# Sliding-window attention with a mixture layer: a written-out order of work and slots in place of the list scheduler, scales on single columns, Strassen's products from step 2

## The chip, the cores and the metric

One core of one Trainium2 chip runs the whole kernel. The metric is device time in microseconds (us); three executions are timed and the median counts. A further execution is profiled, and every row below comes from that one.

## What is computed

```python
B, H, S, SG, D = 8, 8, 512, 32, 64          # batch, heads, local and global tokens, head size
s_g   = q_g @ concat(k_g, k_l).T / sqrt(D)  # 32 global tokens see all 544
out_g = softmax(s_g) @ concat(v_g, v_l)
s_l   = concat(q_l @ k_g.T, where(|i - j| <= 32, q_l @ k_l.T, -1e9)) / sqrt(D)
out_l = softmax(s_l) @ concat(v_g, v_l)
x = concat(out_g, out_l)                    # 4352 tokens of 512
h = x @ w_in                                # 512 -> 2048, both weights come as float64
g = where(h >= 1, h, where(h <= -1, 0, (h + 1)**2 / 4))
out = g @ w_out                             # 2048 -> 512
```

## The kernel before, in words

**Number form.** Every operand of a matmul is scaled by a power of two and split in two float16 halves, high and low, and a product is three matmuls (high-high, low-high, high-low). The weights come as float64 words: `decode`, `signed` (line 590) and `halves` (line 608) make float32 and then the halves from them. To find a scale, the kernel multiplies a tile with itself on PE (a Gram matrix; its largest entry on the diagonal is a squared norm), takes the maximum on DVE, spreads it over the partitions (`all_max`, line 510) and takes the reciprocal.

**Steps.** Eight batches; a batch has two steps of 256 local tokens, so steps 0 to 15, and four batches together have one step for their global tokens. A step's parts have names: `aa` (bit `aa100` is batch 1, tile 0, head pair 0) makes scores on PE, the masked maximum on DVE, exp on ACT, the high half of the probabilities (a cast) on DVE or ACT and the low half (a subtraction) on POOL or DVE, both into a buffer `pb`, and turns `pb` with a transposing DMA. `ab` multiplies the turned probabilities with V; `ax` divides by the sum and turns the result. `m` multiplies with w_in; `act` (line 1133) evaluates the piecewise function on ACT and DVE, and POOL subtracts for the low half. `o` multiplies with w_out and the step's rows are stored. Ahead of these come the loads, the splits of q, k and v (`pq`, `pk`, `pv`), the weights' decoding (`wd`, `od`) and halves (`wh`, `oh`).

**Two forms of `m`.** `moe1` (line 1145) needs 48 matmuls of 128x128 for each of 8 pairs of group and tile, 384 for a step. `moe_f` (line 1199) does it by Strassen's scheme with 7 products of 48 instead of 8, 336 for a step; it needs sums of weight blocks (`combine`, line 1164, and `replace`, line 1183), and more additions on ACT and DVE. `T["fast"]` is the first step that uses it, 3 here.

**What sets the order.** The kernel is written twice over: a first pass records every operation, `segments` (line 198) cuts the record into runs of one engine, and `schedule` (line 252), a list scheduler with a cost for each operation (`cost`, line 151), due times, and a table of 500 hand-set shifts (`LATER`), puts them into one order and gives each tile a slot of the 48 shared SBUF slots of 2 KB (`room`), the 6 of 4 KB (`twin`) or the 8 PSUM banks. All this is done when the program is built. On the chip each engine works through a fixed list, and a second pass in `build` (line 1457) issues it, so nearly every instruction has the line 1474, and loads the line 1476. All DMAs are issued by SP, one after the other; a load also waits for the fifth load before it.

Of the kernel before, what the change touches and what calls it, by code (L numbers as in the profile page):

```python
# [89 lines left out]
def extent(ap, tiles):  # L90

    dims, size = [tuple(d) for d in ap.ap], mybir.dt.size(ap.dtype)
    if tiles[ap.tensor.name][2]:
        return ap.tensor.name, 0, 128, 0, 2048
    row = dims[0][0]
    p0, off = divmod(ap.offset, row) if row else (0, ap.offset)
    n = 1 + sum(abs(st) * (c - 1) for st, c in dims[1:])
    return ap.tensor.name, p0, p0 + dims[0][1], off * size, (off + n) * size


# [10 lines left out]
def shares(engine, op, a, k, tiles):  # L111

    if engine == "gpsimd":
        return op != "memset"
    if engine != "vector" or op in ("memset", "reciprocal", "tensor_reduce"):
        return False
    ins = {"tensor_scalar": a[1:2], "tensor_copy": a[1:2], "scalar_tensor_tensor": [a[1], a[3]] if len(a) > 3 else []}.get(op, a[1:3])
    ins = list(ins) or [k["in0"], k["in1"]]
    held = [x for x in ins if is_ap(x) and not tiles.get(x.tensor.name, (0, 0, 1))[2]]
    return len(held) > 1 or (op in ("tensor_scalar", "tensor_copy") and len(held) == 1 and free(held[0]) > 1)  # L120


def free(ap):
    n = 1
    for d in ap.shape[1:]:
        n *= d
    return n


def stretch(ap):  # L130

    n = 1
    for st, c in reversed([tuple(d) for d in ap.ap][1:]):
        if st != n and c > 1:
            break
        n *= c
    return n * mybir.dt.size(ap.dtype)


def cost(engine, op, a, k, outs, ins, tiles):  # L140

    o = outs[0]
    n = free(o)
    if engine == "tensor":
        if ins and ins[0].dtype == F32:
            return 4 * n / 2.1 + 10, 0
        t = max(28.0, n / 2.4 + 2.5)
        return (t / 4 if o.shape[0] == 32 else t), 0
    if engine == "sync":
        b = o.shape[0] * n * mybir.dt.size(o.dtype)  # L150
        if op == "dma_start_transpose":
            return 1320.0, b / 186.0
        run = min(stretch(x) for x in (o, ins[0]))
        return 600.0, b / (215.0 if run < 512 else 340.0)
    if engine == "scalar":
        ptr = any(free(x) == 1 for x in ins[1:])
        if "accum_out" in k:
            own = 190 if ptr else 95
        elif mybir.dt.size(o.dtype) == 2:
            own = 185 if ptr else 45 if ins[0].tensor.name in tiles and tiles[ins[0].tensor.name][2] else 90  # L160
        else:
            own = 235 if ptr else 135
        return own + n / 1.2 + (93 if "accum_out" in k else 0), 0
    if engine == "gpsimd" and o.dtype == I32:
        return 125 + n * 3.6, 0
    if engine == "gpsimd":
        return (125 + n * (1.93 if len([x for x in ins if free(x) > 1]) > 1 else 1.05) if op != "memset" else 60 + n * 0.82), 0
    big = [x for x in ins if free(x) > 1]
    ps = any(x.tensor.name in tiles and tiles[x.tensor.name][2] for x in big + [o])
    if op == "memset":  # L170
        return 60 + n / 0.96, 0
    if len(big) > 1 or ps or op == "tensor_reduce":
        m = max(free(x) for x in big) if big else n
        return 70 + 60 * len([x for x in ins if free(x) == 1]) + m / 0.96 + (8 if "accum_out" in k else 0), 0
    return 75 + n / (1.92 if n > 16 else 0.96), 0


class Segment:
    __slots__ = ("n", "engine", "calls", "t", "xfer", "after", "before", "new", "uses", "load", "step", "parts", "left", "ready", "prio", "t0", "done")


def segments(steps, tiles, prio, names):

    segs, last = [], {}
    for sn, calls in enumerate(steps):
        cur = None
        for engine, op, a, k in calls:  # L190
            outs, ins = sides(op, a, k)
            t, x = cost(engine, op, a, k, outs, ins, tiles)
            fresh = {tiles[nm][0] for nm in (x.tensor.name for x in outs) if nm in tiles and nm not in last}

            near = [x.tensor.name for x in sides(*cur.calls[-1])[0]] if cur and cur.engine == engine in ("vector", "scalar") else []
            if (cur is None or cur.engine != engine or engine == "sync" or fresh & {tiles[nm][0] for nm in cur.new}
                    or any(x.tensor.name in near for x in ins)):
                cur = Segment()
                cur.n, cur.engine, cur.calls, cur.parts, cur.t, cur.xfer = len(segs), engine, [], [], 0.0, 0.0
                cur.after, cur.before, cur.new, cur.uses = set(), [], [], set()  # L200
                cur.load, cur.ready, cur.prio, cur.step = op == "load", 0.0, prio[sn], names[sn]
                segs.append(cur)
            if engine == "tensor" and not cur.calls and outs[0].shape[0] == 32:
                t += 190.0
            cur.calls.append((op, a, k))
            cur.t += t
            cur.parts.append((t, shares(engine, op, a, k, tiles)))
            cur.xfer += x
            for aps, write in ((ins, False), (outs, True)):
                for ap in aps:  # L210
                    if ap.tensor.name not in tiles:
                        continue
                    nm, p0, p1, b0, b1 = extent(ap, tiles)
                    if nm not in last:
                        assert write, (nm, op)
                        last[nm] = []
                        cur.new.append(nm)
                    cur.uses.add(nm)
                    kept = []
                    for e in last[nm]:  # L220
                        q0, q1, c0, c1, w, who = e
                        if q0 < p1 and p0 < q1 and c0 < b1 and b0 < c1 and (w or write):
                            if who != cur.n:
                                cur.after.add(who)
                            if write and p0 <= q0 and q1 <= p1 and b0 <= c0 and c1 <= b1:
                                continue
                        kept.append(e)
                    e = (p0, p1, b0, b1, write, cur.n)
                    if e not in kept:
                        kept.append(e)  # L230
                    last[nm] = kept
    for g in segs:
        for p in g.after:
            segs[p].before.append(g.n)
# [135 lines left out]
def attention_moe(nc, memory, q_l, k_l, v_l, q_g, k_g, v_g, w_in, w_out, out):  # L370
# [3 lines left out]
    P = 128  # L374
# [1249 lines left out]
```

## Time and profile before

| | us |
|---|---|
| three executions | 939.27, 935.76, 936.0; median 936.0 |
| the profiled execution | 938.49 |
| its span, first to last instruction | 936.8 |
| PE busy in it | 869.6 (93%), 12180 matmuls |
| DVE busy | 778.9 (83%) |
| ACT busy | 636.0 (68%) |
| POOL busy | 425.2 (45%) |
| chain that ended last | PE 63%, DVE 10%, DMA 8%, ACT 5% |

The span is shorter than the profiled execution by 1.7 us, and that execution is 2.5 us above the median. A row names the engine, the operation, what it writes and reads (out<-in, numbers of buffers left out), shapes, the count, busy time and mean length of one, and then how long the engine stood idle before and what ended the wait. A busy PE is not PE at its peak, because matmuls overlap; the granted clock of PE is shown beside it.

### The profile page before, as it was taken

What the parts mean: (1) busy time and instruction counts of PE and PEld (TensorE: products, weight loads), DVE (VectorE), ACT (ScalarE), POOL (GpSimd) and SP (SyncE); (2) the same over time, 40 slices, a digit from 0 to 9 for tenths busy, and PEclk for the clock granted to TensorE, in tenths of its full rate; (3) what the DMA queues carried; (4) which work ended last, traced back from release to release, by engine and by line L of the source; (5) the groups of instructions that cost most, each with busy time, mean ns of one, the idle gap of its engine ahead of it and who ended that gap; (6) DMA issues with size and microseconds to landing.
All of it is one profiled execution on the core that took longest, in us unless ns stands there. A gap on an engine that the chain in (4) does not pass through costs nothing.

```text
span 936.8 us, 30633 instructions
## 1 busy us (share of the span) xinstructions
PE 869.6 (93%) x12180; PEld 648.1 (69%) x12180; DVE 778.9 (83%) x2102; ACT 636.0 (68%) x1530; POOL 425.2 (45%) x447
## 2 busy tenths in 40 slices
PE   2567889989999999999999999999999999999998
PEld 1443857757877686868686768868676777778774
DVE  3889989879888998999678888799879997878462
ACT  2699777768875696688666677668777765566341
POOL 8135475532434534473446344363345352636230
PEclk9788989989999999999999999999999999999999
DMA  8999918988999699979794578949999877364000
GB/s 236 271 230 231 228 24 137 176 168 134 179 175 167 109 181 168 192 127 173 159 182 97 106 161 143 157 70 197 170 182 140 136 131 126 69 123 78 13 24 23
DMA packets 412527, 135.64 MB, mean 145 GB/s; under 512 B 389088, under 2 KB 398304, under 8 KB 412384
## 3 DMA queue, kind: packets, MB, share of 16 engines
q1 hardware_dynamic: 412384, 133.69, 76.7%
q8 instruction: 95, 1.56, 0.7%
q14 instruction: 48, 0.39, 0.1%
HBM read 44.56 MB, written 8.91 MB: 57 GB/s over the span
## 4 chain that ended last, share of the span: by engine, by line
PE 63%; DVE 10%; DMA 8%; ACT 5%; issue 4%; SPq 1%; POOL 1%; ACTq 0%; POOLq 0%; DVEq 0%
PE bank L1474 63%; DVE room L1474 5%; DMA room<-const_pb 3%; ACT room L1474 3%; DVE bank L1474 1%; ACT weights_w L1474 1%; SPq L1474 1%; DMA twin<-in_moe_w_out_dram 1%; DMA room<-in_v_g_dram 1%; POOL room L1474 1%; DMA room<-in_q_l_dram 1%; DVE const_pb L1474 1%; DVE weights_w L1474 1%; ACT junk_junka L1474 1%; DMA room<-in_v_l_dram 1%
## 5 line engine op out<-in xcount | busy, mean ns | idle before, releaser
L1474 PEld LDWEIGHTS <-room 128*128 128x128 f16 (+3 forms) x5056 | 290.2, 99 | 217.2 <-issue 19.3
L1474 PE MATMUL bank<-weights_w,room 128*128 128x512 f16 x1632 | 375.2, 382 | 1.0 <-DVE small_nb L1474 0.4
L1474 POOL TENSOR_TENSOR room<-room,room 128x512 f16<-128x512 f32 (+4 forms) x199 | 222.3, 1124 | 200.1 <-ACT room L1474 182.6
L1474 PEld LDWEIGHTS <-weights_w 128*128 128x128 f16 (+1 forms) x4160 | 231.5, 98 | 39.3 <-DVE weights_w L1474 24.3
L1474 PE MATMUL bank<-room,weights_w 128*128 128x128 f16 (+1 forms) x4032 | 234.7, 216 | 1.5 <-ACT room L1474 0.7
L1474 POOL TENSOR_TENSOR const_pb<-room,const_pb 128x384 f16<-128x384 f32 (+1 forms) x115 | 121.8, 1061 | 214.3 <-DVE const_pb L1474 102.7
L1474 ACT CAST room<-room 128x512 f16<-128x512 f32 (+2 forms) x212 | 121.8, 582 | 84.8 <-DVE room L1474 64.8
L1474 ACT ACTIVATE room<-room,small_nb 128x224 f32<-128x224 f32 (+1 forms) x256 | 117.2, 459 | 46.8 <-DVE small_nb L1474 41.7
L1474 PE MATMUL bank<-room,room 128*128 128x64 f16 (+3 forms) x2688 | 125.3, 197 | 19.6 <-DMA room<-const_pb 11.8
L1474 PE MATMUL bank<-room,twin 128*128 128x128 f16 (+1 forms) x2160 | 123.0, 216 | 0.7 <-DVE room L1474 0.4
L1474 PEld LDWEIGHTS <-twin 128*128 128x128 f16 x2160 | 115.5, 98 | 3.2 <-issue 0.7
L1474 ACT ACTIVATE room<-bank,batch_small_ms 128x512 f32<-128x512 f32 (+1 forms) x114 | 85.1, 751 | 36.7 <-DVE bank L1474 24.7
L1474 DVE CUSTOM_DVE_ANT_0 room<-bank,const_mask,batch_small_q 128x224 f32<-128x224 f32 (+1 forms) x256 | 98.7, 425 | 6.2 <-PE bank L1474 5.8
L1474 ACT ACTIVATE junk_junka<-room 128x512 f16<-128x512 f32 (+2 forms) x110 | 69.0, 628 | 38.9 <-DMA room<-in_q_l_dram 16.4
L1474 DVE SCALAR_TENSOR_TENSOR bank<-bank,batch_small_ms,room 128x512 f32<-128x512 f32 (+1 forms) x114 | 82.0, 721 | 14.7 <-ACT room L1474 14.6
L1474 DVE SCALAR_TENSOR_TENSOR room<-room,batch_small_ms,bank 128x512 f32<-128x512 f32 (+1 forms) x114 | 80.6, 711 | 0.8
L1474 ACT COPY room<-bank 128x512 f32<-128x512 f32 (+2 forms) x98 | 56.2, 589 | 20.3 <-PE bank L1474 18.9
L1474 DVE CAST const_pb<-room 128x448 f16<-128x448 f32 (+1 forms) x109 | 47.6, 438 | 24.1 <-DMA room<-const_pb 20.0
L1474 DVE TENSOR_TENSOR bank<-bank,room 128x512 f32<-128x512 f32 (+1 forms) x60 | 39.4, 658 | 19.3 <-PE bank L1474 18.7
L1474 DVE SCALAR_TENSOR_TENSOR room<-room,batch_small_ms,room 128x512 f32<-128x512 f32 (+1 forms) x60 | 53.2, 887 | 1.3 <-ACT room L1474 0.9
L1474 DVE TENSOR_TENSOR room<-room,room 128x512 f16<-128x512 f32 (+2 forms) x56 | 42.8, 768 | 11.6 <-ACT room L1474 11.2
L1474 ACT ACTIVATION_READ_ACCUMULATOR room<-room,small_nb 128x1 f32 x256 | 48.2, 188 | 0.0
(165 smaller groups left out, 945.4 us busy)
## 6 DMA issues: line engine op xcount, KB each, us to landing
room<-room SPq DMA_DIRECT2D x80, 128.0 KB, 2.8
weights_w<-in_moe_w_in_dram SPq DMA_DIRECT2D x32, 256.0 KB, 4.2
room<-in_q_l_dram SPq DMA_DIRECT2D x32, 256.0 KB, 3.6
twin<-in_moe_w_out_dram SPq DMA_DIRECT2D x32, 256.0 KB, 4.1
out_dram<-room SPq DMA_DIRECT2D x32, 256.0 KB, 3.1
room<-in_k_l_dram SPq DMA_DIRECT2D x24, 256.0 KB, 3.8
room<-in_v_l_dram SPq DMA_DIRECT2D x24, 256.0 KB, 4.4
room<-const_pb SPq DMA_TRANSPOSE x124, 3.6
```

The source lines that it names most:

```text
L1474: getattr(getattr(tc.nc, engine), op)(*a, **k)
```

## The change

The cost functions, the list scheduler and the table of shifts go. In their place stand two tables of numbers, one for the order of all 4635 runs of work and one for the slot of each tile. The settings in `T` that choose an engine for one operation now reach over all 128 head pairs and all 16 steps, where many stopped at the first 16 or 32. Beside that: `fast` is 2; the Gram matrices of w_in, w_out and K add all their blocks into one 128x128 region, where they had 128x512 (for w_in one for eight blocks instead of four, so two reductions in place of four); `moe_scales` and `out_scale` work on one column where the scale is the same for all, and `act` then reads that column. `gram` for q, scaled identities for k and v (`by_pe`, `total`) are written but not used with these settings (`es`, `gramq`).

```diff
-def schedule(segs, tiles, hop, slack, landing, ahead):
...
+def plan(steps, tiles):
+
+    sizes, line = segments(steps, tiles)
+    order = [int(x) for x in ORDER.split()]
+    assert sorted(order) == list(range(len(sizes)))
+    taken = {}
+    for key, nms in line.items():
+        slots = [int(x) for x in SLOTS[key].split()] if key in SLOTS else [0] * len(nms)
...
-        if f % WG == 0:
-            W["n"] = ps_o.tile([P, WG, P], F32, tag="p", name=f"wn{f}")
+        u = f % (2 * WG)
+        if u == 0:
+            W["n"] = ps_o.tile([P, P], F32, tag="p", name=f"wn{f}")
         for k in range(NK):
             x = half[:, k * P:(k + 1) * P]
-            nc.tensor.matmul(W["n"][:, f % WG], x, x, start=(k == 0), stop=(k == NK - 1))
+            nc.tensor.matmul(W["n"], x, x, start=u == 0 and k == 0, stop=u == 2 * WG - 1 and k == NK - 1)
...
+    def gram(tiles, name):
+
+        t = ps_t.tile([P, P], F32, tag="p", name=name)
+        for i, (st, n) in enumerate(tiles):
+            half = st[:n].rearrange("p h d -> p (h d)").bitcast(BF16).rearrange("p (c t) -> p c t", t=2)[:, :, 1]
+            for k in range(NK):
+                x = half[:, k * P:(k + 1) * P]
+                nc.tensor.matmul(t, x, x, start=i == 0 and k == 0, stop=i == len(tiles) - 1 and k == NK - 1)
+        return t
...
-            nc.vector.tensor_reduce(ss, t, axis=AX.XY, op=ALU.max)
+            t = gram(list(d["rawk"].values()), f"kn{b}")
+            nc.vector.tensor_reduce(ss, t, axis=AX.X, op=ALU.max)
...
-        bd, rb, s2, sg, hs, a1, a2 = [t[:, c0:c1] for t in d["ms"][:7]]
+        c = slice(c0, c0 + 1)
+        bd, rb, s2, sg, hs, a1, a2 = [t[:, c] for t in d["ms"][:7]]
...
-    def out_scale(d, gs=None):
+    def out_scale(d, part=3):
...
-        c = slice(g, g + 1)
+        c = g // 2 * 2 if d["first"] else g
+        c = slice(c, c + 1)
...
+ORDER = ("6 7 42 8 5 34 0 4 35 30 1 22 23 24 43 25 26 44 9 45 12 54 13 32 31 82 81 83 84 85 86 89 55 56 57 3 860 1820 280 90 "
...
-T = dict(late=1, fast=3, grams="pp", sqs="aaamaa", cb=200, cbs=5, lk0=4.19, lq0=1.76, lv0=30, sk=12, sq=14,
-         adds="vvvvv1vv1vvvavvv1a1v1aavaavava1v", subs="ppppppvppppvvvpvpppppvvvvpppvppp", glow="ppvppppppppvpppv",
...
-         mags="vaapaaaaaaaaapaaaaapaaaaaaaaaaaa", lows="ppppppvv", halves="aaaaaaaaagacacacdecchccdddfdcbef",
-         shifts="pppapvvpvvvvvvvvvvvvvvvvvpvvvvvv", splits="vvvvvvvvvvvpvvvpvvvpvppp", att=1.35, s0=60, s1=100, s2=254.09,
+T = dict(es="nnnn", gramq="aaaaaaaa", dg="vvvvvvvvvvvvvvv", sid="vvvvv", fast=2, grams="ppaaaaaa", sqs="vaaaaa", cb=200,
...
+         mags="aaappaaaapapappaaaapaaaaaaaaaaaa", lowx="vvvvvvvvvvvvvppvvppvvpvvvvvpvvvvvvvvpvvvvpvppvvpv",
...
+         shifts="pavapvapvvvvvvvvvvvvvvvvvpvvvvvv", splits="vvvvvvvvvvvpvvvpvpvpppvp", att=1.35, s0=60, s1=100, s2=254.09,
```

The engines' lists differ almost everywhere, but their contents little. PE has 48 matmuls of 128x128 fewer. Of the low halves, 33 subtractions of `act` and 23 of `pb` go from POOL to DVE, 10 of `ax` the other way, and 26 casts of `pb` go from DVE to ACT; six copies and six additions come for the earlier Strassen step. SP issues 641 DMAs instead of 639.

**POOL at the start.** `w0` to `w4` are the first blocks of w_in, two instructions for each shift of their low bits; `negid` and `ident` are two diagonal matrices, and `pb0`, `pb1`, `pgb` buffers that are zeroed. Before (the diagonal matrices were POOL's first four instructions, ahead of these):

```order
L1474 MEMSET const_pb0_0_61 128x1024
L1474 MEMSET const_pb1_0_62 128x1024
L1474 MEMSET const_pgb_0_63 128x1280
L1474 MEMSET const_logp_0_64 128x1
L1474 TENSOR_SCALAR weights_w0_0_66<-weights_w0_0_66 128x512 x2
L1474 TENSOR_SCALAR weights_w2_0_68<-weights_w2_0_68 128x512 x2
L1474 TENSOR_SCALAR weights_w1_0_67<-weights_w1_0_67 128x512 x2
```

and now:

```order
L1301 MEMSET const_logp_0_64 128x1
L1301 TENSOR_SCALAR weights_w0_0_66<-weights_w0_0_66 128x512 x2
L1301 MEMSET const_negid_0_84 128x128
L1301 AFFINE_SELECT const_negid_0_84<-const_negid_0_84 128x128
L1301 MEMSET const_ident_0_85 128x128
L1301 AFFINE_SELECT const_ident_0_85<-const_ident_0_85 128x128
```

The two diagonal matrices went behind the shift of `w0`; the shifts of `w1` and `w2` left POOL, for ACT and DVE.

**DVE, the scale of batch 0's K.** `small_amk` holds the norm, `small_dg` the diagonal matrix that PE spreads, `batch_small_sk` the scale that every split of K waits for; `bank` and `weights_w` rows are the decoding of w_in, `q5` the scales of q. Before:

```order
L1474 TENSOR_SCALAR small_amk_0_104<-small_amk_0_104 128x1
L1474 TENSOR_SCALAR small_dg_0_106<-const_negid_0_84,small_amk_0_104 128x128
L1474 TENSOR_SCALAR batch_small_q5_0_111<-batch_small_q5_0_111 128x2
L1474 TENSOR_REDUCE small_wmx_0_103<-bank_3_93 128x1
L1474 TENSOR_SCALAR batch_small_q5_0_111<-batch_small_q5_0_111 128x2
L1474 SCALAR_TENSOR_TENSOR bank_5_108<-bank_5_108,weights_w4_0_70 128x512
L1474 TENSOR_REDUCE small_amk_0_104<-bank_2_91 128x1
L1474 TENSOR_SCALAR batch_small_q5_0_111<-batch_small_q5_0_111 128x2
L1474 TENSOR_SCALAR batch_small_sk_0_107<-small_amk_0_104 128x1
L1474 TENSOR_SCALAR weights_w5_0_71<-weights_w5_0_71 128x512
L1474 RECIPROCAL batch_small_sk_0_107<-batch_small_sk_0_107 128x1
```

and now:

```order
L1301 TENSOR_REDUCE small_amk_0_102<-bank_5_103 128x1
L1301 MEMSET const_ones_0_83 128x128
L1301 TENSOR_SCALAR small_amk_0_102<-small_amk_0_102 128x1 x2
L1301 TENSOR_SCALAR small_dg_0_104<-const_negid_0_84,small_amk_0_102 128x128
L1301 TENSOR_REDUCE small_amk_0_102<-bank_6_105 128x1
L1301 TENSOR_SCALAR batch_small_sk_0_106<-small_amk_0_102 128x1
L1301 RECIPROCAL batch_small_sk_0_106<-batch_small_sk_0_106 128x1
```

The chain now stands in one piece, and nothing of the decoding is between its parts.

**SP, the first turned probabilities of batch 1.** `pb0` is the buffer that `aa100` filled and `pb1` that of `aa101`. Before:

```order
L1476 DMA room_31_129<-in_v_g_dram 32x8x64
L1474 DMA qg_qgb_1_203<-qg_qga_1_202 64x256
L1474 DMA room_28_142<-room_27_144 64x1024
L1474 DMA qg_qgb_1_203<-qg_qga_1_202 64x256
L1476 DMA room_20_115<-in_v_l_dram 128x8x64
L1476 DMA room_0_92<-in_v_l_dram 128x8x64
L1476 DMA room_44_159<-in_v_l_dram 32x8x64
L1474 DMA room_40_195<-room_5_98 64x1024
L1476 DMA room_44_159<-in_v_g_dram 32x8x64
L1474 DMA_TRANSPOSE room_23_119<-room_37_140 128x8x128
L1474 DMA_TRANSPOSE room_18_114<-const_pb0_0_61 128x8x128
L1474 DMA_TRANSPOSE room_33_137<-const_pb1_0_62 128x8x128
```

and now:

```order
L1301 DMA room_46_159<-room_35_138 64x1024
L1301 DMA room_40_193<-room_6_113 64x1024
L1303 DMA room_5_112<-in_q_l_dram 128x8x64
L1303 DMA room_29_129<-in_v_l_dram 32x8x64
L1301 DMA_TRANSPOSE room_2_86<-room_23_136 128x8x128
L1301 DMA_TRANSPOSE room_31_140<-const_pb0_0_61 128x8x128
L1301 DMA_TRANSPOSE room_16_116<-const_pb1_0_62 128x8x128
```

Fewer loads of the next batch's V stand right ahead of the two transposes. On PE, between the scores of `aa100` and the first matmul that reads what it had turned, stood one group of 48 of `m`, three groups of 12 of `o` and six other pairs' scores; now it is four of `m`, five of `o` and seven pairs' scores.

## Rows read from the trace of the kernel before

**Rows 1.** The page: busy time and share of each engine, and the 40 slices of 23.4 us of PE's busy share and of its granted clock, in tenths.

```profile
PE 869.6 (93%) x12180; PEld 648.1 (69%) x12180; DVE 778.9 (83%) x2102; ACT 636.0 (68%) x1530; POOL 425.2 (45%) x447
...
PE   2567889989999999999999999999999999999998
...
PEclk9788989989999999999999999999999999999999
```

**Rows 2.** Stretches of the span: start and end, length, then busy time (and instructions) of PE, PE's weight loads, DVE, ACT and POOL, PE's granted clock, the DMA engines' busy share and GB/s.

```profile
0.00:60.00 60.00, 26.63 (x191) 19.32 (x192) 40.46 (x116) 32.80 (x68) 25.42 (x44) 0.84 0.99 255
60.00:165.00 105.00, 88.85 (x1219) 64.08 (x1218) 96.95 (x272) 87.59 (x194) 62.57 (x62) 0.93 0.80 158
165.00:225.00 60.00, 54.39 (x728) 39.76 (x727) 49.82 (x162) 43.70 (x124) 21.57 (x22) 0.94 0.89 162
225.00:328.00 103.00, 101.48 (x1396) 78.38 (x1396) 90.20 (x225) 72.57 (x176) 46.55 (x48) 1.00 0.90 157
328.00:937.00 609.00, 598.21 (x8651) 446.60 (x8649) 501.47 (x1332) 399.32 (x971) 269.11 (x273) 1.00 0.72 128
```

**Rows 3.** What PE waited for in the first 60 us: us in total, times, the longest.

```profile
PE bank L1474 <- DVE weights_w L1474: 21.6, 4, 15.4
PE bank L1474 <- DMA room<-room: 4.2, 1, 4.2
PE bank L1474 <- DVE small_w L1474: 3.6, 1, 3.6
```

**Rows 4.** The same from 165 us to the end.

```profile
PE bank L1474 <- DMA room<-const_pb: 9.9, 6, 4.4
PE bank L1474 <- DVE room L1474: 0.7, 2, 0.4
```

**Rows 5.** The timeline around 195 us, start, length, what, count, of PE, POOL and SP, and the stretch around it as in rows 2.

```profile
194.65 0.59 PE L1474 MATMUL bank<-room,room 128*128 128x128 f16 x12
199.64 2.21 PE L1474 MATMUL bank<-room,room 128*128 128x64 f16 x36 [4.40 <-DMA room<-const_pb]
201.66 3.97 PE L1474 MATMUL bank<-weights_w,room 128*128 128x512 f16 x12
...
189.99 0.92 POOL L1474 TENSOR_TENSOR const_pb<-room,const_pb 128x384 f16<-128x384 f32 x1 [0.29 <-DVE const_pb L1474]
...
196.27 2.65 SPq L1474 DMA_TRANSPOSE room<-const_pb  x2
...
187.40:210.80 23.40, 19.00 (x208) 12.23 (x206) 17.50 (x67) 15.05 (x51) 8.20 (x8) 0.85 0.86 168
```

**Rows 6.** The timeline of PE between 232 and 244 us, and the page's group of 128-column products.

```profile
235.85 0.52 PE L1474 MATMUL bank<-room,room 128*128 128x64 f16 x12
236.20 2.84 PE L1474 MATMUL bank<-room,weights_w 128*128 128x128 f16 x48
...
239.24 2.75 PE L1474 MATMUL bank<-weights_w,room 128*128 128x512 f16 x12
...
L1474 PE MATMUL bank<-room,weights_w 128*128 128x128 f16 (+1 forms) x4032 | 234.7, 216 | 1.5 <-ACT room L1474 0.7
```

**Rows 7.** The timeline of the first 16 us: POOL's diagonal matrices and its shifts of w_in's first three blocks, DVE's decoding of them and PE's first matmul.

```profile
0.80 0.21 POOL L1474 MEMSET const_negid<- 128x128 f16 x1 [0.29 <-POOLq L1608]
...
1.59 0.29 POOL L1474 TENSOR_SCALAR_AFFINE_SELECT const_ident<-const_ident 128x128 f16<-128x128 f16 x1
...
8.06 8.78 POOL L1474 TENSOR_SCALAR weights_w<-weights_w 128x512 f32<-128x512 uint16 x6
...
10.80 0.70 DVE L1474 SCALAR_TENSOR_TENSOR bank<-room,weights_w 128x512 int32<-128x512 int32 x1 [5.93 <-POOL weights_w L1474]
...
14.68 1.28 DVE L1474 SCALAR_TENSOR_TENSOR weights_w<-weights_w,bank 128x512 int32<-128x512 int32 x2
...
15.41 0.64 PE L1474 MATMUL bank<-weights_w 128*128 128x128 bf16 x4 [15.41 <-DVE weights_w L1474]
```

**Rows 8.** The timeline of DVE for batch 0's K: the two reductions, the diagonal matrix and the reciprocal.

```profile
18.33 0.69 DVE L1474 TENSOR_REDUCE small_amk<-bank 128x1 f32<-128x512 f32 x1
...
20.45 0.48 DVE L1474 TENSOR_SCALAR small_dg<-const_negid,small_amk 128x128 bf16<-128x128 f16 x1
...
22.92 0.28 DVE L1474 TENSOR_REDUCE small_amk<-bank 128x1 f32<-128x128 f32 x1
...
24.40 0.16 DVE L1474 RECIPROCAL batch_small_sk<-batch_small_sk 128x1 f32<-128x1 f32 x1
```

**Rows 9.** Stretches as in rows 2, for the transfers of the start.

```profile
0.00:93.70 93.70, 50.92 (x466) 33.69 (x467) 71.61 (x214) 65.80 (x141) 45.29 (x63) 0.85 1.02 242
93.70:117.10 23.40, 19.91 (x363) 19.28 (x360) 21.74 (x54) 17.14 (x37) 11.25 (x11) 1.00 1.05 228
117.10:140.50 23.40, 20.40 (x266) 12.89 (x264) 20.04 (x60) 17.93 (x42) 16.55 (x16) 0.85 0.15 24
```

**Rows 10.** Groups by shape: the low half of `act` on DVE and on POOL, w_in's norms, a reduction of 128x128, and the additions of Strassen's scheme.

```profile
L1474 DVE TENSOR_TENSOR room<-room,room 128x512 f16<-128x512 f32 x42 | 33.0, 790 | 11.0 <-ACT room L1474 10.7
L1474 POOL TENSOR_TENSOR room<-room,room 128x512 f16<-128x512 f32 x137 | 172.2, 1264 | 161.5 <-ACT room L1474 151.3 <-issue 5.5 <-PE bank L1474 4.3
L1474 DVE TENSOR_REDUCE small_wmx<-bank 128x1 f32<-128x512 f32 x4 | 2.7, 678 | 0.0
L1474 DVE TENSOR_REDUCE small_amv<-bank 128x1 f32<-128x128 f32 x8 | 2.2, 276 | 0.8 <-PE bank L1474 0.8
L1474 DVE TENSOR_TENSOR bank<-bank,room 128x512 f32<-128x512 f32 x52 | 35.9, 693 | 16.1 <-PE bank L1474 15.7
```

**Rows 11.** The instructions on the buffers `pb` and their lengths in ns, shortest/median/longest.

```profile
L1474 POOL TENSOR_TENSOR const_pb<-room,const_pb x115: 908/1035/1772, 58.5 to 844.1; 128x384 f16<-128x384 f32 x58, 128x448 f16<-128x448 f32 x57
L1474 DVE CAST const_pb<-room x109: 340/379/1347, 109.8 to 843.6; 128x448 f16<-128x448 f32 x55, 128x384 f16<-128x384 f32 x54
...
L1474 ACT CAST const_pb<-room x15: 494/516/565, 58.0 to 239.0; 128x384 f16<-128x384 f32 x8, 128x448 f16<-128x448 f32 x7
L1474 DVE TENSOR_TENSOR const_pb<-room,const_pb x9: 534/615/870, 130.4 to 232.9; 128x448 f16<-128x448 f32 x5, 128x384 f16<-128x384 f32 x4
```

**Rows 12.** A stretch late in the run, as in rows 2.

```profile
749.40:772.90 23.50, 23.50 (x309) 17.82 (x308) 23.50 (x63) 15.43 (x37) 12.43 (x11) 1.00 0.71 131
```

More of the change, by code (lines that the diff above doesn't have):

```diff
@@ L108, in sides @@
     return outs, ins
[L111 to L120, printed above, removed]
@@ L123, in free @@
[L123 to L175, printed above, removed]
@@ L178, with segments @@
[L178 to L188, printed above, removed]
+def segments(steps, tiles):
+    segs, line, seen = [], {}, set()
+    for calls in steps:
         cur = None
         for engine, op, a, k in calls:
[L191 to L201, printed above, removed]
-                segs.append(cur)
[L203 to L234, printed above, removed]
-    return segs
@@ L343, in deadlines @@
-def deadlines(segs, order, hop, slack, landing):
-    late, t = {}, 0.0
-    for n in reversed(order):
-        g = segs[n]
-        took = g.t + (g.xfer + landing if g.engine == "sync" else 0.0)
-        x = t - took if g.engine == "tensor" else 0.0
-        for b in g.before:
-            c = segs[b]
-            wait = (hop if c.engine != g.engine else OWN) + (slack if c.engine == "tensor" and g.engine != "tensor" else 0.0)
-            x = min(x, late[b] - wait - took)
-        if g.engine == "tensor":
-            t = x
-        late[n] = g.prio = x
@@ L359, in plan @@
-def plan(steps, tiles, prio, names, hop, slack, landing, ahead):
-    segs = segments(steps, tiles, prio, names)
-    if T["late"]:
-        deadlines(segs, [g.n for g in segs], hop, slack, landing)
-    for g in segs:
-        g.prio += LATER.get(g.step, 0.0) * (1.0e3 if T["late"] else 1.0)
-    order, taken, _ = schedule(segs, tiles, hop, slack, landing, ahead)
-    return order, segs, taken
+            outs, ins = ([x.tensor.name for x in s] for s in sides(op, a, k))
+            new = [nm for nm in dict.fromkeys(outs) if nm in tiles and nm not in seen]
@@ new lines, in segments @@
+            if (cur is None or engine == "sync" or cur[0] != engine or cur[1].intersection(tiles[nm][0] for nm in new)
+                    or engine in ("vector", "scalar") and any(nm in cur[2] for nm in ins)):
+                cur = [engine, set(), [], 0]
+                segs.append(cur)
+            for nm in new:
+                seen.add(nm)
+                line.setdefault(tiles[nm][3], []).append(nm)
+                cur[1].add(tiles[nm][0])
+            cur[2] = outs
+            cur[3] += 1
@@ new lines, in segments @@
+    return [n for _, _, _, n in segs], line
+def plan(steps, tiles):
[5 more added lines that the diff above has]
+        slots = [int(x) for x in SLOTS[key].split()] if key in SLOTS else [0] * len(nms)
+        assert len(slots) == len(nms) and max(slots) < (ROOMS[key][1] if key in ROOMS else tiles[nms[0]][1])
+        taken.update(zip(nms, slots))
+    return order, sizes, taken
```

300 lines of the change are left out of this document (120 added, 180 removed), and 358 rows, old and new, of tables (LATER, ORDER, SLOTS).

## The prediction

> **What bounds the kernel now.** I read the page's shares first: PE is busy for 869.6 us of 936.8, DVE for 83%, ACT and POOL less [rows 1]. That makes PE the bound, but not everywhere: in the slices PE fills from 2 to 9 tenths over the first quarter of the span, and its clock is below full only there. So I cut the span in stretches [rows 2]. In the first 165 us PE is idle for 165 - 26.6 - 88.9 = 49.5 us; from 165 to 328 us for 7.1; in the last 609 us for 10.8, of which 3.8 are the store behind the last matmul. Three quarters of all PE's idle time lies in the start, and what follows is a PE stream with few holes.
>
> Then, what ended PE's waits. In the first 60 us it is DVE, which decodes the weights [rows 3]; from 60 to 165 us DVE is busy for 97 of 105 us [rows 2], and DMA engines are full until 117 us and nearly empty after it [rows 9], so the loads of both weights are over there. From 165 us on nearly the whole wait is for one kind of transfer, the turned probabilities: 9.9 us in 6 waits [rows 4]. The longest shows how it comes about [rows 5]. POOL had written the low half of a `pb` by 191 us; SP, which issues everything in turn, came to the transpose at 196.3; PE had run out of other work at 195.2 and went on at 199.6, at half speed: 12 matmuls of 512 columns took 3.97 us there and 2.75 later [rows 5, 6], with a granted clock of 0.85 over that stretch.
>
> Both lists are fixed before the chip starts. "Explicit order instead of a scheduler" is therefore no mechanism: what counts is which instruction stands where, and I take the change by its places.
>
> **Strassen from step 2.** 336 products instead of 384, 48 fewer of 128 columns. A group of 4032 such is busy for 234.7 us, 0.058 us each [rows 6]: 48 x 0.058 = **-2.8 us**, all on PE's path, since step 2 lies after the start. The sums of weights that it needs are the same as before, only earlier; they hide beside PE as long as DVE has room (below).
>
> **The waits for turned probabilities.** I counted PE's work between the scores of each of the 128 head pairs and the first matmul that reads their turned probabilities, in the two orders, at 0.215 us for 512 columns, 0.056 for 128 and 0.029 for 64 (lengths of [rows 6] less the last matmul's tail, by their counts). The median goes from 18.4 to 25.3 us, and the pairs with less than 14 us from 33 to 9, most of them now in batch 0. For the pair of rows 5 it goes from 13 to 27 us, where 4.4 were missing. Nearly all that PE lost late is thus covered: I take -8 of the 9.9; the bounds are -9.9 - 3.9 (every visible wait after 165 us, [rows 2]: 7.1 + 7.0 idle) and 0 (the same wait at another pair). The half-speed stretch behind the longest wait goes with it: 3.97 - 2.75 = 1.2 us on those 12 and some on the short ones, **-1.5**. Together **-9.5 us**.
>
> **The start.** Three edits. (1) POOL makes the two diagonal matrices, some 1 us, behind the shift of `w0` instead of ahead, and leaves `w1` and `w2` to ACT and DVE. Before, six shifts took POOL from 8.1 to 16.8 us, DVE merged `w2` ahead of finishing `w0`, and PE began at 15.4 [rows 7]. Now: shift done at some 9.8, two merges at 0.70, one sign step at 0.64, PE at some 12: 3.4 us earlier. (2) The chain to K's scale took from 19.0 (reduction done) to 24.6 us [rows 8], over 5.5 us, because decoding stood between its parts; the parts themselves are 0.48 + 0.28 + 0.16 and three of some 0.15, with a small matmul, so some 2.3 us: 3.2 earlier. The reduction falls from 0.69 to 0.28 by its width. (3) DVE gets less to do: two w_in norms at 0.68 and two at 0.28 fewer by width, two K norms and three of w_out the same way [rows 10, 8], 4.2 us in all. That makes 3.4 + 3.6 + 4.2 = 11.2 us if all were on one path. They aren't: up to 117 us transfers run without a pause, and ahead of the last piece of w_out SP issues 28.2 MB now instead of 27.6, 0.6 MB or 2.6 us more at 228 GB/s [rows 9]. I take a little over half, **-6.5**; the bounds are +2.6 (transfers alone decide) and -14 (half of the 27.6 us for which DVE is idle in those 165 us, [rows 2]).
>
> **What is added.** DVE takes 33 subtractions of `act` at 0.79 us and 23 of `pb` at some 0.62, and six additions at 0.69, +44 us; it loses 10 of `ax` at 0.79, 26 casts at 0.38 to 0.44, and some 11 us of reductions and of scales on one column [rows 10, 11]: about +15 in the sum, 779 to 794 us. POOL loses about 45 us. ACT gains 26 casts at 0.52 and six copies, +17. ACT and POOL have room. DVE has it in the sum, but the step-2 part is dense: between the last `o` of step 1 and the end of step 2's `m`, where PE has 50 us of work, DVE has 47 now and had 41 (counted over the same pieces). I charge **+2** there, with bounds 0 and +8 (47 us at DVE's share of 83%, [rows 1], are 57, less 50). For new waits at other slots and in SP's new order I charge **+1**, bounds 0 and +4.4, one wait as long as the longest.
>
> A DVE cast of `pb` takes 0.34 us at best and 1.35 at worst, a DVE subtraction 0.53 to 0.87, while ACT's cast stays within 0.49 to 0.57 [rows 11]. The Trainium skill (SBUF — State Buffer, Who interferes with whom) says that GpSimd and a VectorE instruction with two SBUF inputs, or in its two-port mode, take one pair of ports from each other for a whole instruction, and that ScalarE never waits for it. By that rule a subtraction that leaves POOL unblocks others, the added time on DVE is less than 15 us, and the +2 would be 0, an end of 920.7 in place of 922.7 for the profiled execution; these spreads agree with it, but no row shows the two engines' pairs one by one, so I keep +2.
>
> **Sum.** -2.8 - 9.5 - 6.5 + 2 + 1 = -15.8. Against the profiled execution's 938.5 that is 922.7; it stood 2.5 us above the median of 936.0, so I forecast **920**.
>
> **Rivals.** *The start pays in full and the late holes close*: -2.8 - 13.8 - 2 - 14 = -32.6, some 903. For it speaks that DVE is idle for a sixth of the start; against it that transfers run full there. *Only the product count helps*: the holes come back at other pairs and the start is set by transfers; -2.8, or about 933. For it speaks that batch 0 keeps distances of 8 to 18 us and that the loads are the same. *DVE becomes the bound, slower*: 794 us at the share that DVE reached before, 83.1%, is 955, or 953 for the median. It decides once DVE's share can't rise above 794/936 = 85%. For it speaks that DVE waits for ACT and PE in every chain; against it, that DVE stood at 92% from 60 to 165 us and at 100% in a late stretch with PE just as full [rows 2, 12]. *The written order doesn't fit the chip*, so that SP or an engine waits at the head of its list while others could go: it would be seen in the start first, at some 10 us, 940 to 946; it is the same kind of list as before, so this has little weight and shares the last chance below.
>
> **Chances.** The forecast, about 908 to 931: 0.70. All pays, below 908: 0.07. Only the products, 931 to 938: 0.14. DVE as the bound or a list that fits badly, 941 and above: 0.09. A measurement of this kernel can tell about 0.5%, 4.7 us, from no change: faster means below 931.3 and slower above 940.7. I put 0.02 of the third case below the line: faster 0.79, same 0.13, slower 0.08. For 8 in 10 the range leaves out the ends of the first and the last cases: 906 to 935.
>
> **What would show it.** Right: PE's count falls by 48; the waits of PE for `room<-const_pb` after 165 us fall from 9.9 to some 2 us; PE's first matmul at some 12 us; K's reciprocal earlier than 24.6; PE's idle time to the last `o` of step 0 falls from 49.5 to 40 to 45 us; DVE busy about 794 us and POOL about 380. Wrong: PE waiting for DVE between 225 and 330 us for more than 3 us, the clock below 1.00 after 250 us, or a start as long as before with the last load of w_out past 118 us.

## The result, and the profile of the changed kernel

The changed kernel takes **944.2 us** (median of 20 runs, 939.5 to 949.6) where the kernel before takes 936.5 (20 runs, 933.3 to 940.8): ratio **1.0076**, 95% interval [1.0058, 1.0095]. It is slower by some 7 us; the forecast was 920.

The profiled execution is its fastest, 939.5 us with a span of 937.7. The page of it, in the columns of [rows 1]:

```profile
PE 866.4 (92%) x12132; PEld 647.6 (69%) x12132; DVE 763.1 (81%) x2128; ACT 646.0 (69%) x1574; POOL 371.0 (40%) x411
...
PE   2577989999999998999899999999999999999998
...
PEclk9969999999999999999999999999999999999999
```

PE has 48 matmuls fewer and its busy time fell by 3.2 us, but the span didn't. The start is better than before: the third, fifth and ninth slices are fuller, and PE's clock is at 9 tenths or more from the fourth slice on. The loss lies further back: slices 16 and 20 fall to 8 tenths. In stretches, with the columns of [rows 2], the changed kernel:

```profile
165.00:338.00 173.00, 169.21 (x2465) 131.20 (x2464) 154.24 (x460) 135.76 (x352) 66.09 (x72) 1.00 0.88 158
338.00:480.00 142.00, 130.58 (x1793) 96.17 (x1792) 110.49 (x307) 95.47 (x245) 58.68 (x59) 0.98 0.81 150
480.00:937.00 457.00, 447.27 (x6401) 331.05 (x6397) 358.13 (x962) 287.89 (x703) 156.57 (x170) 1.00 0.65 115
```

and a second profile of the kernel before, cut at the same places:

```profile
165.00:338.00 173.00, 166.53 (x2345) 127.97 (x2344) 151.34 (x423) 127.82 (x333) 72.52 (x76) 0.99 0.90 163
338.00:480.00 142.00, 139.97 (x2014) 104.50 (x2011) 129.15 (x364) 106.75 (x268) 71.04 (x73) 1.00 0.94 166
480.00:937.00 457.00, 447.65 (x6422) 332.08 (x6419) 363.82 (x932) 282.22 (x673) 193.29 (x195) 1.00 0.65 115
```

From 338 to 480 us PE is idle for 142 - 130.6 = 11.4 us where it was idle for 2.0. What it waited for behind 165 us (as in [rows 4]):

```profile
PE bank L1301 <- DMA room<-const_pb: 9.5, 5, 3.2
PE bank L1301 <- DMA room<-room: 6.7, 6, 1.9
PE bank L1301 <- DVE room L1301: 2.9, 7, 0.7
```

The turned probabilities are back with 9.5 us. New is what SP, which issues all transfers, itself waits for behind 165 us (us in total, times, longest): its own earlier transfers, in these four rows 52 us in 31 waits,

```profile
SPq L1301 <- DMA room<-room: 27.0, 18, 3.2
...
SPq L1301 <- DMA out_dram<-room: 14.6, 8, 3.6
...
SPq L1303 <- DMA out_dram<-room: 6.5, 3, 2.7
...
SPq L1303 <- DMA room<-room: 4.1, 2, 3.2
```

where the kernel before has, in its second profile,

```profile
SPq L1474 <- DMA room<-room: 3.0, 2, 2.3
```

**A measure for the rest: the lag.** I count PE's work by the lengths of the prediction (0.215 us for a matmul of 512 columns, 0.056 for 128, 0.029 for 64, others alike; 837.1 us in all before, 834.4 now) and take it from the time at which it is done. The lag grows only where PE idles or runs slowly. The third profile of the change is that of e8, the change with its slots at other addresses.

| lag at | 165 us | 338 us | 480 us | 920 us |
|---|---|---|---|---|
| before, two profiles | 72.4, 72.9 | 84.3, 83.3 | 88.6, 87.3 | 95.8, 95.5 |
| the change, three profiles | 65.8, 68.1, 67.7 | 71.8, 75.3, 74.8 | 88.8, 92.5, 90.3 | 99.4, 104.6, 101.1 |
| the change with roomy slots (e1, below) | 70.1 | 74.8 | 81.4 | 88.8 |

At 338 us the change leads by some 10 us of lag and 2.7 of work. Then it loses 28 to 920 us, where the kernel before loses 12.

### The profile page after: what moved, and what is told of

The parts are those of the page before. It is cut to its first block, busy times and chain, and to the rows that moved or that the text cites. A ratio compares the mean times of both kernels' runs of the same rounds, so it can differ in the third digit from the quotient of the medians.

```text
span 937.7 us, 30437 instructions
## 1 busy us (share of the span) xinstructions
PE 866.4 (92%) x12132; PEld 647.6 (69%) x12132; DVE 763.1 (81%) x2128; ACT 646.0 (69%) x1574; POOL 371.0 (40%) x411
## 5 line engine op out<-in xcount | busy, mean ns | idle before, releaser
L1301 PEld LDWEIGHTS <-room 128*128 128x128 f16 (+1 forms) x5048 | 290.5, 99 | 225.0 <-issue 17.3
L1301 POOL TENSOR_TENSOR room<-room,room 128x512 f16<-128x512 f32 (+4 forms) x183 | 194.9, 1074 | 263.7 <-ACT room L1301 219.8
L1301 PEld LDWEIGHTS <-weights_w 128*128 128x128 f16 (+1 forms) x3968 | 222.7, 99 | 37.2 <-DVE weights_w L1301 19.1
L1301 PE MATMUL bank<-room,weights_w 128*128 128x128 f16 (+1 forms) x3840 | 225.4, 218 | 5.4 <-DMA room<-room 4.5
L1301 POOL TENSOR_TENSOR const_pb<-room,const_pb 128x448 f16<-128x448 f32 (+1 forms) x92 | 96.2, 1046 | 209.9 <-DVE const_pb L1301 94.5
L1301 ACT CAST room<-room 128x512 f16<-128x512 f32 (+2 forms) x215 | 122.4, 582 | 81.9 <-DVE room L1301 57.2
L1301 PE MATMUL bank<-room,room 128*128 128x64 f16 (+3 forms) x2688 | 125.3, 197 | 15.8 <-DMA room<-const_pb 9.7
L1301 PE MATMUL bank<-room,twin 128*128 128x128 f16 (+1 forms) x2304 | 132.0, 216 | 1.5 <-ACT room L1301 1.4
L1301 PEld LDWEIGHTS <-twin 128*128 128x128 f16 x2304 | 123.1, 98 | 3.9 <-DMA room<-room 1.6
L1301 DVE CUSTOM_DVE_ANT_0 room<-bank,const_mask,batch_small_q 128x224 f32<-128x224 f32 (+1 forms) x256 | 99.4, 427 | 18.5 <-PE bank L1301 17.5
L1301 DVE TENSOR_TENSOR room<-room,room 128x512 f16<-128x512 f32 (+2 forms) x78 | 58.1, 753 | 7.8 <-ACT room L1301 7.6
L1301 DVE SCALAR_TENSOR_TENSOR room<-room,batch_small_ms,room 128x512 f32<-128x512 f32 (+1 forms) x64 | 47.8, 747 | 4.1 <-ACT room L1301 3.8
L1301 DVE CAST const_pb<-room 128x448 f16<-128x448 f32 (+1 forms) x83 | 32.3, 390 | 16.2 <-DMA room<-const_pb 8.3
(168 smaller groups left out, 949.6 us busy)
```

The source lines that it names most:

```text
L1301: getattr(getattr(tc.nc, engine), op)(*a, **k)
```

## The experiments

I call a tile's slot tight when the tile enters it less than 0.3 us after its last user left it (by a trace's times), and roomy otherwise. Each ratio is to runs of the kernel before that were timed beside the run.

| run | median us | ratio to before, 95% interval |
|---|---|---|
| the change | 944.2 | 1.0076 [1.0058, 1.0095] |
| e1 roomy slots | 927.3 | 0.9893 [0.9873, 0.9913] |
| e2 two orders | 927.6 | 0.9901 [0.9881, 0.9921] |
| e3 before, tight slots | 943.4 | 1.0069 [1.0048, 1.0090] |
| e4 tight for SP | 935.4 | 0.9980 [0.9960, 1.0000] |
| e5 tight for engines | 934.2 | 0.9959 [0.9936, 0.9982] |
| e6 60 subtractions on POOL | 941.8 | 1.0034 [1.0015, 1.0054] |
| e8 slots renamed | 944.0 | 1.0074 [1.0048, 1.0100] |
| e9 banks too | 927.4 | 0.9904 [0.9882, 0.9926] |
| e10 two orders, other seam | 929.5 | 0.9927 [0.9906, 0.9948] |
| e11 27 of the 60 on POOL | 932.4 | 0.9945 [0.9924, 0.9966] |

**e1: the slots alone.** ORDER stays. `SLOTS["room"]` gets other numbers for the tiles first written after 165 us; at one place of SP's list this reads

```diff
 L1301 DMA out_dram<-room_17_115 128x512
-L1303 DMA room_17_115<-in_v_g_dram 32x8x64
+L1303 DMA room_24_127<-in_v_g_dram 32x8x64
 L1301 DMA_TRANSPOSE room_40_193<-const_pb1_0_62 128x8x128
```

(the numbers of the other two rows change as well; left as they were for the eye). In the change the load goes into the buffer that the store right ahead of it still reads.

> The change with its order untouched; only the slots of the 48 shared buffers differ for tiles first written after 165 us: of the buffers that are free, the one that has been free longest (by the times of the change's trace). Before it 133 of 1213 tiles stood in a buffer left less than 0.3 us earlier, now 41; in the kernel before the change it was 14 of 1199. Theory S (slots): SP stands in front of buffers that another transfer or PE has only just left (my count: 112 us of SP's gaps in the change, 6 before), the turned probabilities behind it come late, and that is where the gain of the first 340 us goes; then this run gives back at least 6 us, 930 to 938, and SP's waits for its own DMAs fall from 48 us to under 20. Theory O (order): the sequence itself puts low halves and transposes late from batch 3 on, whatever buffer they use; then 941 to 947.

Measured: 927.3, all of the loss and more, even below theory S's 930 to 938; SP's waits for its own transfers fall from 55.8 us (34 waits) to 12.9 (9). Theory S holds, theory O falls. The place above in the timeline of the change: POOL's low half, SP's store, load and transpose, PE's wait and its next matmuls.

```profile
341.62 0.92 POOL L1301 TENSOR_TENSOR const_pb<-room,const_pb 128x384 f16<-128x384 f32 x1 [3.87 <-DVE const_pb L1301]
...
347.78 1.20 SPq L1301 DMA_DIRECT2D out_dram<-room  x1
...
350.80 0.33 SPq L1303 DMA_DIRECT2D room<-in_v_g_dram  x1
...
351.21 1.23 SPq L1301 DMA_TRANSPOSE room<-const_pb  x1
...
354.48 1.46 PE L1301 MATMUL bank<-room,room 128*128 128x64 f16 x20 [2.66 <-DMA room<-const_pb]
...
355.75 6.32 PE L1301 MATMUL bank<-weights_w,room 128*128 128x512 f16 x24
```

The low half is written at 342.5. SP's store is out at 349.0, the load behind it comes only at 350.8, and the transpose, which has nothing to do with either, stands behind the load: 351.2. PE waits 2.66 us for it, and the 24 matmuls of 512 columns behind the wait take 6.32 us. From 354.3 to 357.7 us, and so for 1.95 us of these matmuls, the granted clock is at half:

```profile
354.30:357.70 3.40, 3.22 (x25) 2.00 (x26) 1.58 (x7) 0.58 (x2) 1.19 (x2) 0.50 1.28 251
```

From 338 to 354.3 us, ahead of that, PE had been busy for 11.7 of 16.3 us. With roomy slots, the same instructions:

```profile
345.71 0.92 POOL L1301 TENSOR_TENSOR const_pb<-room,const_pb 128x384 f16<-128x384 f32 x1 [4.95 <-DVE const_pb L1301]
...
346.53 0.58 SPq L1301 DMA_DIRECT2D out_dram<-room  x1
...
347.21 0.38 SPq L1303 DMA_DIRECT2D room<-in_v_g_dram  x1
...
347.69 1.23 SPq L1301 DMA_TRANSPOSE room<-const_pb  x1
...
353.79 5.34 PE L1301 MATMUL bank<-weights_w,room 128*128 128x512 f16 x24
```

The load follows the store's issue by 0.10 us instead of 1.82, and the transpose comes 3.5 us earlier: 1.7 by this wait, 0.6 by the store's shorter issue, 1.2 from what lies ahead. (From low half to transpose it is 1.1 us instead of 8.7, but most of the 8.7 SP spent on four transposes ahead in its list, and the low half came 4.1 us later in e1.) PE doesn't wait for the transpose here, it had been busy for 15.2 of the 15.8 us from 338 us on, its clock stays at 1.00, and the same 24 matmuls take 5.34. In sum, the two longest of PE's waits behind 165 us in e1,

```profile
PE bank L1301 <- DVE room L1301: 3.2, 6, 1.5
PE bank L1301 <- DMA room<-const_pb: 3.0, 3, 1.5
```

the longest of SP's waits for its own transfers there,

```profile
SPq L1301 <- DMA room<-room: 5.3, 4, 2.0
SPq L1303 <- DMA out_dram<-room: 3.2, 1, 3.2
```

and the stretches: 4.35 us of idle PE from 338 to 480 instead of 11.4.

```profile
165.00:338.00 173.00, 170.23 (x2484) 132.26 (x2482) 156.19 (x464) 134.17 (x349) 67.24 (x72) 1.00 0.89 163
338.00:480.00 142.00, 137.65 (x1937) 102.08 (x1935) 119.47 (x330) 102.24 (x261) 60.91 (x61) 1.00 0.92 159
480.00:937.00 457.00, 439.54 (x6285) 324.84 (x6282) 353.51 (x944) 283.14 (x692) 153.49 (x169) 1.00 0.63 112
```

The tightness can be counted in the list of SP's instructions, without a chip: transfers into a buffer that one of the two transfers right ahead reads are 0 in the kernel before, 32 in the change, 5 in e1.

**e8: the same waits at other addresses.** Each slot number n becomes p(n), p a permutation of the 48.

> The change with the numbers of its 48 shared slots permuted: tiles that shared a slot still do, at another address, so every wait for a slot stays as it was. Theory S (the 17 us are waits for buffers just left): the change's own time, 942 to 947. Theory M (the roomy slots helped because the tiles came to lie at other addresses, so that accesses collide less): a time of its own, below 938 or above 950.

Measured: 944.0, with 51 us of SP's waits for its own transfers, as in the change. At these other addresses nothing changes: the cost goes with whom a tile shares its slot, not with where it lies.

**e3: the kernel before made tight.**

```diff
-                    taken[nm] = slots[key].pop(0)
+                    taken[nm] = slots[key].pop(2 * len(slots[key]) // 3 if key == "room" else 0)
```

> The kernel before, same order of every engine; of the free shared buffers it takes one two thirds down the queue instead of the one that has been free longest. By its own trace's times 145 of 1199 tiles then stand in a buffer left under 0.3 us before (14 as it was; 133 in the change). Theory S: the same kind of waits appear, and the time rises by 6 us or more, 942 to 952. Theory O: within 3 us of 936.5.

Measured: 943.4, 6.5 us more at the same order. So the cost doesn't hang on the new order: the scheduler's rule, the buffer that has been free longest, was worth that much in the kernel before. The waits are of another kind, though: SP waits for its own transfers for 10 us there (3 and 4 in the two profiles of the kernel before), but for PE's matmuls for 62 us instead of 36 and 29.

**e4 and e5: whose slots.** Other numbers in `SLOTS["room"]` again, dealt behind 165 us from the longest free on for one kind of tile and from further down the row for the other.

> The change's order, slots dealt anew behind 165 us so that only tiles which a transfer of SP writes first are tight: 51 of these 340 stand in a buffer left under 0.3 us before (49 in the change, 8 in the run with roomy slots), and only 12 of the tiles that ACT, DVE or POOL write first (78 in the change, 27). Theory S1 (the cost is SP's: one queue, and a transfer that waits for its buffer holds all behind it, the turned probabilities among them): most of the 17 us comes back, 937 to 946. Theory S2 (the cost is the engines', whose casts and exps wait for a buffer that PE has just read): 926 to 931.

> The mirror of it: 79 of the tiles that ACT, DVE or POOL write first are tight (78 in the change), and 2 of the 340 that SP writes (49 in the change). Theory S1: 926 to 931, SP has no slot to wait for. Theory S2: most of the 17 us comes back, 937 to 946. If both kinds hurt alike, 933 to 938 in each of the two runs.

Measured: 935.4 and 934.2. Neither S1 nor S2: the third case, both alike. By the ratios, of the 17 us between e1 and the change (1.0076 - 0.9893 of 937) SP's tiles make 8.2 and the engines' 6.2, together 14.4. I had expected SP's alone. These are prices of two other dealings and not shares of the change's own waits. In e4 SP waits for its own transfers for only 17 us (13 in e1, 56 in the change); what grew is its wait for PE, in e1

```profile
SPq L1301 <- PE bank L1301: 27.7, 29, 2.2
```

and in e4:

```profile
SPq L1301 <- PE bank L1301: 60.8, 47, 4.9
```

It also loses its time elsewhere: from 338 to 480 us the lag grows by 7.0 us in e4, as in e1 (6.6) and not as in the change (17), and then by 15 to 920 us (7.4 in e1). For e5 there is no trace to set beside these. How the change's 17 us divide among its own waits is therefore not shown.

**e2 and e10: the order of the change up to 338 us, then the order of the kernel before.** ORDER gets its second part from the kernel before (step and place in the step decide), and the tables of choices lose their late entries, as in

```diff
-casts="aaaaaaaaaavaaaaavvavvaavavvvvavvvaavvvavvvavvvvvvvvvaaavvvvvvvvaavvavvvv...
+casts="aaaaaaaaaavaaaaavvavvaavavvvvavvvaavvvavvvavvvvvvvvvvvvvvvvvvvvvvvvvvvvv...
```

> The change's own order and choices for everything that it starts in its first 338 us; from there on the order of the kernel before and its choices of engines (the late entries of adds, casts, subs, lows, glow and lowx set back), slots by longest free after 165 us. At 338 us the change is 12.8 us ahead of the kernel before in lag and has 2.7 us less work. Theories S and O both say that this lead is real and is lost by what stands behind 338 us: 936.5 - 15.5 = 921, 917 to 927. Theory P (the lead is borrowed): PE ran ahead of the loads, preparations and DVE, which set the pace, and the lead is given back under any order: 932 to 940.

> The run of two orders (927.6) with one step more of SP's own list: SP follows the change until 343 us instead of 338, so the swaps of q for batch 3 stand where the change has them. At the seam PE waited 4.0 us for these swaps, and its lag grew by 7.1 us from 338 to 360 us. If the lead of the first 338 us is real and only the seam ate it, 920 to 924; if another wait takes its place, as theory P (PE ran ahead of what sets the pace) would have it, 926 to 929.

Measured: 927.6 and 929.5. By the ratios that is 9 and 7 us better than before, short of the 921 that a kept lead would give. The lag shows where: 74.8 to 81.9 from 338 to 360 us in e2, then 8.6 more to 920 us. At the seam PE waits 4.0 us for the swaps of batch 3's q; in e10, with these swaps earlier, it waits 1.4 there and 4.7 for ACT right after. Two lists made for different surroundings don't fit at the joint, and my repair moved the wait. Theory P isn't excluded by these two; e1 excludes it, since there the lead of 338 us (8.5 to 9.5 us of lag) is 6.7 to 7.0 at the end.

**e9: banks as well.** `SLOTS["bank"]` dealt like `SLOTS["room"]`.

> The run with roomy slots (927.3), its slots dealt a second time with that run's own times, and the 8 PSUM banks dealt in the same way too: of 453 tiles in banks 29 instead of 43 then stand in one left under 0.3 us before. If banks cost as shared slots do, 922 to 925; if banks are no limit, as every matmul waits for its bank's readers anyway, 925 to 929.

Measured: 927.4, as e1. Dealt anew together with the slots, the banks gain nothing that can be measured.

**e6 and e11: the low halves back to POOL**, in e1 and at their places, for 27 `pb` (23 net, as four others had gone the other way) and 33 `act`; e11 changes `subs` alone.

```diff
-subs="ppppppvppppvvvppvpppvppvvpppppvvvppppvppppppppppp..."
-glow="ppvpppvppppvvvpvpvppvpppp...
+subs="ppppppvppppvvvpppppppppvvpppppppppppppppppppppppp..."
+glow="ppvppppppppvpppvpppppppp...
```

> The run with roomy slots (927.3), and 60 subtractions of low halves back on POOL as in the kernel before: 33 of act and 27 of pb, each at its place in the order. By the trace's lengths DVE loses 33 x 0.79 + 27 x 0.58 = 42 us and POOL gains 33 x 1.26 + 27 x 1.04 = 70. Theory A (these moves cost DVE time and are worth nothing for the rest, as the prediction charged them): 924 to 928, DVE busy 766 - 42 = 724. Theory B (POOL is the slower and later of the two, the move is part of the gain): 930 to 936. Theory C (DVE and POOL hold each other up, so DVE's other work gets longer when POOL has more): DVE busy well over 724, 735 to 750, whatever the time.

> The run with roomy slots (927.3), with the 27 subtractions of pb alone back on POOL; the 33 of act stay on DVE. With all 60 back it was 941.8, 14.4 us more. Theory Q (the probabilities' own subtraction decides, as it stands on the way from scores to the transpose, some 0.45 us longer on POOL and behind what POOL has queued): 937 to 942. Theory R (the subtractions of act decide: each blocks POOL for 1.26 us, with the probabilities' ones behind it, and m's results wait for it): 927 to 932.

Measured: 941.8 and 932.4. Theory B for the first, beyond its 930 to 936, and theory C for DVE's busy time, 743.8: by the ratios the moves to DVE are worth 13 us in this order, more than e1 gains over the kernel before in all (10). For the second neither Q nor R alone: 5 for `pb`, the other 8, by difference, for `act`. Where they act can be seen for `pb`. What PE waited for from 165 to 225 us in e11,

```profile
PE bank L1301 <- DMA room<-const_pb: 2.3, 1, 2.3
PE bank L1301 <- DVE room L1301: 2.0, 2, 1.6
PE bank L1301 <- DVE small_nb L1301: 1.2, 1, 1.2
```

and in e1,

```profile
PE bank L1301 <- DVE small_nb L1301: 1.2, 1, 1.2
PE bank L1301 <- DVE room L1301: 0.8, 2, 0.4
```

From 165 to 225 us the lag grows by 8.4 us in e11 and by 3.2 in e1; in the kernel before by 8.7. PE's list is the same in e11 and e1. By name the turned probabilities stay low all the same: behind 165 us PE waits for them for 3.9 us in e11 and 3.8 in e6 (3.0 in e1, 9.9 before), and for DVE's `room` tiles for 4.9 and 6.7 (3.2 in e1, 0.7 before). And SP waits for the low halves again, behind 165 us 33.5 us in e1,

```profile
SPq L1301 <- POOL const_pb L1301: 33.5, 22, 5.0
```

and 61.4 in e6:

```profile
SPq L1301 <- POOL const_pb L1301: 61.4, 39, 7.0
```

How the subtractions of `act` cost their 8 us I haven't traced.

**e0 and e7: the change and the kernel before once more,** for the lag.

> The change itself once more, for a second profile: the first one shown was its fastest of 20 (939.5, median 944.2). All theories: 940 to 948; if the additional time lies behind 338 us, the lag at 338 us is again 71 to 73 us and the rest is lost in waits for turned probabilities; theory P would have it spread over the start as well.

> The kernel before once more, for a second profile of its start. Four profiles of the change's start stood at a lag of 65.8, 68.1, 70.1 and 70.1 us at 165 us, and the kernel before at 72.4. If the start's gain is the 6.5 us of the prediction, its lag here is 74 to 76 again or at least 72; if the start differs from run to run more than from kernel to kernel, it is 69 to 71.

Measured: 944.7 and 938.1. Both lags are in the table above: the loss behind 338 us comes again, though the lag at 338 us is 75.3 and not 71 to 73, and the start's gain too, as 72.9 stands against 65.8 to 70.1.

## Why the prediction was wrong, step by step

**New waits at other slots, +1: the step that failed.** I gave the slots no more than "one wait as long as the longest", 0 to +4.4, because I read ORDER and saw SLOTS as names. They cost 17 us (e1 against the change), more than the whole forecast gain. A slot table decides which instruction waits for which; SP, with one list for all, passes each wait on. The trace of before couldn't show the cost, since its rule hardly made such waits; the two lists of SP could: 0 and 32 transfers into a buffer just left. Of the rivals the badly fitting list named this time, 940 to 946, but looked for it in the start. Of the signs that I had named for a wrong forecast one came up: the clock fell below 1.00 behind 250 us, to 0.98 from 338 to 480 us, at half for 3.4 us from 354.3 and again from 456.7. It is no cause of the loss by itself, as e8's profile stands at 1.00 there and its lag grows by 15 us all the same. The other signs lie ahead of 330 us, where the change was ahead.

**Turned probabilities, -9.5: too large by some 3, the reason incomplete.** With the slots out of the way the waits of PE for them fell from 9.9 to 3.0 us (forecast: some 2), and from 165 to 338 us the lag grows by 4.7 us (e1) and 5.8 (e9) where it grew by 11.9 and 10.4, so some -6. But I credited the longer distance between scores and their use on PE alone. e11 has that distance, and from 165 to 225 us it loses what the kernel before lost (8.4 and 8.7 us), if in part by waits of other names; only with the 27 subtractions taken from POOL is the stretch covered (3.2). Whether they would do without the distance, no run shows. The half-speed stretch at 197 us is gone in the change (1.00 from 165 to 338 us, 0.99 in the second profile of before).

**The start, -6.5.** Right in its signs, but smaller: PE's first matmul at 12.95 us (forecast some 12; [rows 7]: 15.41), K's reciprocal at 22.75 ([rows 8]: 24.40, so 1.65 us earlier where I took 3.2).

```profile
12.95 1.24 PE L1301 MATMUL bank<-weights_w 128*128 128x128 bf16 x8 [12.95 <-DVE weights_w L1301]
...
22.75 0.16 DVE L1301 RECIPROCAL batch_small_sk<-batch_small_sk 128x1 f32<-128x1 f32 x1
```

PE is idle for 45.7 us to 165 us (forecast 40 to 45), and for 48.9 in e1, which has the same start. Over nine profiles with this start the lag at 165 us is 65.8 to 70.1, mean 68.0, against 72.4 and 72.9: -4.6, some 2 us less than I took. That the three edits make it isn't shown: e3, the order of before with other slots from its first tile on, stands 2.4 to 2.8 us lower than the two profiles of before as well.

**Strassen, -2.8.** 12180 to 12132 matmuls, 837.1 to 834.4 us of work: right.

**DVE, +2: the wrong sign.** I forecast 794 us; it is 763.1, and 766 in e1. (The bound of +8 there is a slip: 57 less 50 is 7.) DVE's instructions got shorter: in one of its large groups an instruction took 930 ns before

```profile
L1474 DVE SCALAR_TENSOR_TENSOR room<-room,batch_small_ms,room 128x512 f32<-128x512 f32 x52 | 48.4, 930 | 1.1 <-ACT room L1474 0.9
```

and takes 782 now.

```profile
L1301 DVE SCALAR_TENSOR_TENSOR room<-room,batch_small_ms,room 128x512 f32<-128x512 f32 x56 | 43.8, 782 | 4.1 <-ACT room L1301 3.8
```

Over all forms, change of the mean times the count, that is some 35 us. e6 shows in the one order how much of it hangs on POOL: I took 42 us of instructions from DVE and gave POOL 62, and DVE's busy time fell by 22. The pages of e1

```profile
PE 863.5 (93%) x12132; PEld 646.3 (70%) x12132; DVE 765.9 (83%) x2128; ACT 645.5 (70%) x1574; POOL 370.2 (40%) x411
```

and e6:

```profile
PE 866.5 (92%) x12132; PEld 646.2 (69%) x12132; DVE 743.8 (79%) x2068; ACT 644.6 (69%) x1574; POOL 432.5 (46%) x471
```

In e6 the group above takes

```profile
L1301 DVE SCALAR_TENSOR_TENSOR room<-room,batch_small_ms,room 128x512 f32<-128x512 f32 x56 | 46.0, 821 | 4.7 <-ACT room L1301 4.4
```

and in e1 784 ns, in e11 (POOL busy for 397 us) 777. The rule that I cited in the prediction (the Trainium skill, SBUF — State Buffer, Who interferes with whom) agrees in kind with e6: what goes to POOL lengthens DVE's other instructions, in sum by some 13 us. But e6 has POOL busier than before, 432.5 us against 425.2, and stays far from 930 ns, so POOL's total explains only a part; the rest came with the new order, by what in it isn't shown. I quoted the rule and kept the +2; by e6 the 60 moved subtractions as a whole were a gain of 13 us. The rival that made DVE the bound took its 794 us for granted.

**The sum without the slots.** e1 is 0.9893 of the kernel before, -10.0 us. By the lag: -4.6 for the start, some -6 from 165 to 338 us, -2.7 of work and +1.7 behind 338 us (14.0 and 13.1 in e1 and e9, 11.5 and 12.2 before), -11.6. The forecast of -15.8 would have been some 6 us too good there as well.

**What stays open.** Why the change's median lies some 2.5 us above the mean of its three profiled executions (e8's among them); which of the change's waits carry the 17 us, and what an engine's tight slot costs one by one; whether a better seam would bring e2 to 921. The best version measured is e1, with e2 and e9 within their intervals: 927.

## What to carry to other kernels

A table of buffers is a second order of the work: before believing a hand-written one, count for each queue the transfers into a buffer that one of the two transfers ahead still reads, and deal out the buffer that has been free longest. The count is a warning and no measure: it is 5 in e1, 10 in e4 and 3 in e5, and e5 is 6 us slower than e1 by the tight slots of its engines. Put a price on what an edit lets an engine wait for, even where its rows look like names. And to cover a latency, look also at which engine's list holds its last piece; distance on PE without that wasn't enough here.

## What the runs showed of the hardware

A load into a buffer that the transfer just ahead reads stood 1.82 us behind that transfer's issue; into another, free one it was 0.10. The same group of DVE's instructions took 930 ns before (POOL busy for 425 us), 782 in the change (371), 777 in e11 (397) and 821 in e6 (432), so that POOL's total alone doesn't set it. Behind a wait of PE of 2.66 us, 24 matmuls of 512 columns took 6.32 us instead of 5.34, as the granted clock was 0.50 from 354.3 to 357.7 us there and 1.00 in e1: this wait cost more than its own length.
